# Fewer, larger transposing transfers in a fused attention and token-mixing kernel: z by overlapping twos, the last row block by two groups, keys by the stretch

## The chip, the cores and the metric

The kernel runs on one core of one Trainium2 chip. The metric is the device time of one execution in microseconds (us), lower is better; several executions are timed and their median is taken. One more execution is recorded by the hardware profiler, and every row of a profile below is of such an execution. PE is the matmul engine (PEld its weight loads), DVE, ACT and POOL are the vector, scalar and general engines, and SP issues most of the DMA transfers.

## What is computed

Eight batches of 3200 rows; u and v have 256 columns, z has 64.

```python
def _attn_ref(u, v, z):
    scale = 1.0 / S
    scores = scale * np.matmul(z, z.transpose(0, 2, 1))
    attn = np.maximum(scores, 0.0) ** 2
    out = np.matmul(attn, v)
    return u * out                       # this is x of the second part

def _moe_ref(x, w_q, w_k, w_out):
    wq = x @ w_q                         # queries, 64 columns
    wk = x @ w_k                         # keys, 64 columns
    W_tok = (1 / sqrt(64)) * np.einsum('bsd,btd->bst', wq, wk)
    mixed = np.einsum('bst,btd->bsd', W_tok, x)
    return np.maximum(mixed, 0.0) @ w_out
```

There is no softmax in either part. The second part is computed as queries times the small matrix "keys transposed times x" (64 x 256), which the kernel calls the heads.

## The kernel before

**Tiling.** A batch's 3200 rows are 25 row blocks of 128. They are grouped into seven groups: six of 512 rows (four blocks) and a last one of 128 rows (the row block 24, `LASTG`). A *tile* (b, gi, t) is the score block of row block t against the 512 (or 128) columns of group gi, after relu and square. Tiles are made in pairs: two score matmuls, one on the upper and one on the lower 64 rows of PE (`scores`, L224), into one PSUM tile; then relu on DVE or ACT (`first_stage`, L247 or L243); then the square on POOL or ACT into a buffer `at` (`second_stage`, L262 or L260), of which there are `NAT` = 15. Because two matmuls run side by side on 64 rows each, the turned z (`zT`) must hold the 64 values of z twice, in both halves of the 128 partitions.

**Symmetry.** The score matrix is symmetric, so the tile of group gi against block t also gives, transposed, the tile of t's group against gi's rows. For near groups (`is_turned`: at most two groups further, or the last group) the squared tile is transposed by a DMA on SP's queue (L282, buffers `tt1`, `tt2`, and `ttl` for the last row block) instead of being computed again. In the order of pairs, the tile of row block 24 stands as the last of a group's turned ones, paired with whatever comes next, and is transposed alone, 512 columns wide.

**Accumulation.** For each group the products of squares and v are added up in PSUM (`second_product`, L316), 10,000 matmuls of 64x256 in all. This is the bulk of PE's work. A finished group is multiplied by u (`gate`, L353), transposed by DMA (`turn_x`, L377), projected to queries and keys (L394), and cast to fp16 on ACT (L407) into `qk`, which holds queries in one half of the partitions and keys in the other, the halves swapped for the second half of a group.

**Keys and heads.** Each group's `qk` is transposed as a whole by one DMA (`turn_keys`, L412, 53 of them) although only its keys are used. When all groups of a stretch (groups 0 to 2, then 3 to 6) have their keys turned, the head products run on PE (`heads`, L421). After the second stretch the mixing of the batch (L457) and the output projection (L509) follow, among the next batch's work.

**z of the next batch.** `load_z` brings it densely on POOL's queue (with a cast to fp16); two DVE copies (`double_z`, L150, 128x1600 each) write every value twice, side by side; five transposing DMAs (`turn_z`, L156, five row blocks each) make `zT`. The first batch's z is doubled by casts and transposed on PE (L126) instead.

**Order.** The order of all instructions is written at build time by a planner inside the kernel. It keeps a clock for each engine and for SP and the DMA engines with assumed costs (for a transposing DMA, 1.28 us of SP and 0.21 us of DMA per row block), and chooses at each step between a new pair, a product that is ready, and extra work. `move(ready, due, issue, takes, ...)` queues a DMA for SP with a time from which it may go and one by which it is due. On the chip each engine then runs its list in that order and waits on semaphores. SP issues in order as well: a transfer that waits for its data holds everything behind it.

Of the kernel before, what the change touches and what calls it, by code (L numbers as in the profile page):

```python
# [9 lines left out]
FP16 = mybir.dt.float16  # L10
# [6 lines left out]
def kernel(  # L17
# [37 lines left out]
    NK = 5  # L55

    consts = ctx.enter_context(tc.tile_pool(name="consts", bufs=1))
    pz = ctx.enter_context(tc.tile_pool(name="pz", bufs=1))
# [3 lines left out]
    pk = ctx.enter_context(tc.tile_pool(name="pk", bufs=NK))  # L62
# [7 lines left out]
    pq = ctx.enter_context(tc.tile_pool(name="pq", bufs=10))  # L70
# [16 lines left out]
    zT, vs, us, xs, xTs, qks, ks, hacc, hx, hss, rts, zds = ({} for _ in range(12))  # L87
# [9 lines left out]
    zd0 = pz.tile([P, NT, 2, dqk], FP16, tag="zd", name="zd")  # L97
    vs[0] = pv.tile([P, NT, D], FP16, tag="v_sb", name="v_sb")
    zT[0] = pzt.tile([P, S], FP16, tag="zT2", name="zT2")
# [41 lines left out]
    zdense, ztimes = {}, []  # L141

    def load_z(b):
        zdense[b] = pz.tile([P, NT, dqk], FP16, tag="zn", name="zn")
        nc.gpsimd.dma_start(out=zdense[b][:], in_=rows(z, b))

    def double_z(b, half):
        if half == 0:
            zds[b] = pz.tile([P, NT, 2, dqk], FP16, tag="zd", name="zd")
        nc.vector.tensor_copy(out=zds[b][:, :, half, :], in_=zdense[b][:])  # L150

    def turn_z(b, i):
        ztimes.append((b, i))
        if i == 0:
            zT[b] = pzt.tile([P, S], FP16, tag="zT2", name="zT2")
        nc.sync.dma_start_transpose(  # L156
            out=zT[b][:].rearrange("p (n s) -> p n s", s=P)[:, 5 * i : 5 * i + 5, :],
            in_=zds[b][:, 5 * i : 5 * i + 5, :, :].rearrange("p n a k -> p (n a k)"),
        )

# [33 lines left out]
    def is_turned(gi, gj):  # L194
        return gi < gj and (gj <= gi + FAR or gj == LASTG)
# [4 lines left out]
    tiles, ends = [], {}  # L200
    for b in range(B):
        for gi in range(NG):
            near = [t for t in range(NT) if is_turned(gi, group_of(t))]
            own = [
                t for t in range(NT) if t not in near and not is_turned(group_of(t), gi)
            ]
            if b == 0 and gi == 0:
                order = own + near
            elif len(tiles) % 2:
                order = own[:1] + near + own[1:]  # L210
            else:
                order = near + own
            tiles += [(b, gi, t) for t in order]
            ends[b, gi] = len(tiles)
    NTILE = len(tiles)
    NPAIR = NTILE // 2
    made, turned = {}, {}

    def scores(p):
        assert len(ztimes) >= 5 * tiles[2 * p + 1][0] and p_chunk(p) in z_at, (p, clock, len(ztimes), z_at)  # L220
        sc = ps_tile("sc")
        for h, (b, gi, ti) in enumerate(tiles[2 * p : 2 * p + 2]):
            gs, gw = starts[gi], widths[gi]
            nc.tensor.matmul(  # L224
                out=sc[:, h, 0:gw],
                lhsT=zT[b][top(h), ts(ti, P)],
                rhs=zT[b][top(h), ds(gs, gw)],
                start=True,
                stop=True,
            )  # L230
        return sc
# [21 lines left out]
    def second_stage(p, g, on_act):  # L253
        at = pat.tile([P, 2 * W], FP16, tag="at", name="at")
        at0 = 0
        for hs, w in pieces(p):
            n = hs.stop - hs.start
            out = at[:, at0 : at0 + n * w].rearrange("p (n w) -> p n w", w=w)
            if on_act:
                nc.scalar.square(out=out, in_=g[:, hs, 0:w])  # L260
            else:
                nc.gpsimd.tensor_mul(out=out, in0=g[:, hs, 0:w], in1=g[:, hs, 0:w])  # L262
            at0 += n * w
        at0, blocks = 0, []
        for tile_ in tiles[2 * p : 2 * p + 2]:
            b, gi, ti = tile_
            made[tile_] = (at, at0)
            gj = group_of(ti)
            if is_turned(gi, gj):
                blocks.append((b, gi, gj, ti - starts[gj] // P, 1, at0, at0 + widths[gi]))  # L270
            at0 += widths[gi]
        if len(blocks) == 2 and blocks[0][:3] == blocks[1][:3] and blocks[1][3] == blocks[0][3] + 1:
            blocks = [blocks[0][:4] + (2, blocks[0][5], blocks[1][6])]

        def turn(b, gi, gj, n0, nn, c0, c1):
            if (b, gi, gj) not in turned:
                kind, nr, bufs = ("l", 1, 8) if gj == LASTG else (gj - gi, 4, gj - gi + 2)
# [4 lines left out]
            nc.sync.dma_start_transpose(out=out[:, 4 * n0 : 4 * (n0 + nn), :], in_=at[:, c0:c1])  # L282

        return [(x, lambda x=x: turn(*x)) for x in blocks]


# [3 lines left out]
    def weights(b, gi, ti, j):  # L290
        if (b, gi, ti) in made:
            at, at0 = made[b, gi, ti]
            return at[:, ds(at0 + j * P, P)]
        gj = group_of(ti)
        return turned[b, gj, gi][:, j, ti - starts[gj] // P, :]
# [33 lines left out]
    def gate(g):  # L329
# [4 lines left out]
        if b == B - 1 and gi == GRAM:  # L334
            spare = pz.tile([P, NT, 2, dqk], FP16, tag="zd", name="xd")
            spare = spare[:].rearrange("p n a k -> p (n a k)")
# [64 lines left out]

    def projections_out(b, gi, ps):
        xTs.pop((b, gi))
        n = min(2, widths[gi] // P)
        qks[b, gi] = pq.tile([P, 2, HW], FP16, tag="qk", name="qk")
        nr = len(halves(gi))
        nc.scalar.copy(out=qks[b, gi][:, 0:nr, 0 : n * P], in_=ps[:, 0:nr, 0 : n * P])  # L407

    def turn_keys(b, gi):
        nn = widths[gi] // P  # L410
        ks[b, gi] = pk.tile([P, 4, 2, dh], FP16, tag="kx", name="kx")
        nc.sync.dma_start_transpose(  # L412
            out=ks[b, gi][:, 0:nn, :, :].rearrange("p n a h -> p n (a h)"),
            in_=qks[b, gi][:].rearrange("p r s -> p (r s)")[:, 0 : nn * P],
        )

    def heads(b, gis, ps):
        todo = [(gi, n) for gi in gis for n in range(widths[gi] // P)]
        for i, (gi, n) in enumerate(todo):
            for r in range(2):  # L420
                nc.tensor.matmul(  # L421
                    out=ps[top(i % 2), r, 0:D],
                    lhsT=ks[b, gi][top(r), n, 1 - n // 2, :],
                    rhs=x_rows(b, gi, n)[top(r), :, :],
                    start=(i < 2),
                    stop=(i >= len(todo) - 2),
                )
        for gi in gis:
            del xs[b, gi], ks[b, gi]
# [23 lines left out]
    def mix(b, gi, banks):  # L453
        n = min(2, widths[gi] // P)
        for db in range(ND):
            for r in halves(gi):
# [3 lines left out]
                    rhs=qks[b, gi][top(r), r, 0 : n * P],  # L460
# [233 lines left out]
    def block_landed(t, p, b, gi, gj, nn):  # L694
# [5 lines left out]
        if blocks[b, gi, gj] == widths[gj] // P:  # L700
            for n in range(widths[gi] // P):
                row_at[b, gj, starts[gi] // P + n] = t + 0.5

    def use_keys(b, gi):
# [7 lines left out]
        n = widths[gi] / P  # L712
        if b < last or gi < GRAM:
# [4 lines left out]
        close_slot(slot, done)  # L718

    FIRST_HEADS = range(3)  # L720

    def keys_landed(b, gi):
        keyed.append((b, gi))
        for gis in FIRST_HEADS, range(3, NG if b < last else GRAM):
            if gi in gis and all((b, i) in keyed for i in gis):
                add_extra(clock[PE] + 0.5, "heads", lambda gis=gis: use_heads(b, gis))

    def use_heads(b, gis):
# [7 lines left out]
        if gis is FIRST_HEADS:  # L736
            return
# [73 lines left out]
    def batch_begun(b, t):  # L811
        if b + 1 < B:
            t += 6 if b == 0 else 0
            at_time(t + 6, lambda: (load_z(b + 1), push(3.0)))
            for half in range(2):
                at_time(
                    t + 18 + 3 * half,
                    lambda half=half: (double_z(b + 1, half), give(DVE, clock[PE], 0.98)),
                )
            for i in range(5):  # L820
                move(t + 24 + 6 * i, t + 40 + 6 * i, 1.28, 1.05, lambda i=i: turn_z(b + 1, i))
# [147 lines left out]

    make_identity(nc, ident)  # L970
# [31 lines left out]
    while stages or work:  # L1002
# [18 lines left out]
        able = p < NPAIR and z_at[p_chunk(p)] <= now and (p < NAT or all_used(p - NAT) and turned_at.get(p - NAT, 0.0) <= now and not out_of.get(p - NAT))  # L1021
# [131 lines left out]
```

## Time and profile before

| | us |
|---|---|
| median of three timed runs | 775.47 |
| lowest and highest | 773.03, 776.76 |
| the profiled execution | 773.32 |
| its span, first to last instruction | 771.5 |
| granted clock of PE, share | 0.998 |
| PE busy in the span | 753.5 |
| POOL, ACT, DVE busy | 563.9, 496.7, 461.4 |

The profile is of one execution. Its page gives busy time by engine, the chain of work that ended last, and groups of instructions by source line; each group's row has count, busy time, the mean of one in ns, and the idle time of the engine before them with what ended it. Further views list waits, DMA transfers with the time from issue to landing, and the instructions in order of time.

### The profile page before, as it was taken

How to read it: one execution, taken by the hardware profiler on the slowest of the kernel's cores; microseconds unless marked ns; L12 is line 12 of the kernel's file. 1: busy time of each engine (PE TensorE's matmuls, PEld its weight loads, DVE VectorE, ACT ScalarE, POOL GpSimd, SP SyncE). 2: the span in 40 equal slices, each digit the busy share in tenths (PEclk: the TensorE clock that was granted, in tenths of full speed). 3: DMA queues.
4: the chain of work that ended last, by engine and by line, in shares of the span. 5: the costliest groups of instructions: out<-in, count | busy, mean ns of one | idle time of the engine just before them, and what ended most of it. 6: DMA issues, size and time to landing. Idle time of an engine off the chain costs nothing.

```text
span 771.5 us, 28734 instructions
## 1 busy us (share of the span) xinstructions
PE 753.5 (98%) x12707; PEld 654.1 (85%) x12707; DVE 461.4 (60%) x496; ACT 496.7 (64%) x650; POOL 563.9 (73%) x363
## 2 busy tenths in 40 slices
PE   6999999999999999999999999999999999999996
PEld 4788889888888889988898898889988899888884
DVE  5675466555586465655556554755577756566544
ACT  5565766755676666777666666776657466775425
POOL 7896686885888477776788567875787768878840
PEclk9999999999999999999999999999999999999999
DMA  8899999999999999999999999999999999998636
GB/s 196 139 191 144 185 176 180 153 189 228 194 194 169 202 205 189 205 147 229 178 209 167 175 198 206 178 197 159 220 188 194 154 189 185 226 201 166 166 82 235
DMA packets 309806, 142.49 MB, mean 185 GB/s; under 512 B 287408, under 2 KB 291376, under 8 KB 309680
## 3 DMA queue, kind: packets, MB, share of 16 engines
q1 hardware_dynamic: 302624, 124.34, 88.7%
q0 software_dynamic: 6768, 15.98, 15.7%
q8 instruction: 99, 1.62, 0.9%
q10 hardware_dynamic: 288, 0.33, 0.1%
q14 instruction: 27, 0.22, 0.1%
HBM read 59.64 MB, written 26.21 MB: 111 GB/s over the span
## 4 chain that ended last, share of the span: by engine, by line
PE 91%; DMA 3%; DVE 2%; POOL 1%; issue 1%; SPq 1%; ACT 0%; DVEq 0%; POOLq 0%; ACTq 0%
PE acc L316 67%; PE sc L224 13%; PE fo L509 5%; PE qk L394 3%; PE hd L421 2%; DMA tt<-at 2%; PE mx L457 2%; DVE g L247 1%; PE fo L484 1%; DMA v_sb<-in_v_dram 1%; POOL at L262 1%; SPq L282 0%; DMA z<-in_z_dram 0%; DVE fo L557 0%; PE xtx L577 0%
## 5 line engine op out<-in xcount | busy, mean ns | idle before, releaser
L262 POOL TENSOR_TENSOR at<-g 128x1024 f16<-128x1024 f32 (+1 forms) x279 | 520.0, 1879 | 172.1 <-DVE g L247 125.0
L316 PE MATMUL acc<-v_sb,at 64*128 64x256 f16 x7312 | 494.8, 270 | 3.7 <-DMA v_sb<-in_v_dram 2.2
L247 DVE TENSOR_SCALAR g<-sc 128x1024 f32<-128x1024 f32 (+1 forms) x292 | 348.4, 1206 | 213.9 <-PE sc L224 197.4
L316 PEld LDWEIGHTS <-at 64*128 64x128 f16 x7312 | 387.1, 94 | 58.7 <-issue 5.0
L243 ACT ACTIVATE g<-sc 128x1024 f32<-128x1024 f32 (+2 forms) x176 | 173.1, 988 | 119.4 <-PE sc L224 107.3
L260 ACT ACTIVATE at<-g 128x1024 f16<-128x1024 f32 (+2 forms) x189 | 191.0, 1019 | 18.1 <-DVE g L247 14.8
L224 PE MATMUL sc<-zT 64*128 64x512 f16 x920 | 176.5, 380 | 2.9 <-DVE g L247 1.6
L316 PE MATMUL acc<-v_sb,tt 64*128 64x256 f16 x2304 | 167.3, 269 | 0.3 <-DMA tt<-at 0.3
L316 PEld LDWEIGHTS <-tt 64*128 64x128 f16 x2304 | 124.0, 94 | 16.7 <-issue 0.9
L353 DVE TENSOR_TENSOR x_sb<-acc,u_sb 128x512 f16<-128x512 f32 x92 | 59.0, 683 | 26.2 <-PE acc L316 23.2
L562 ACT ACTIVATE fo<-fo 128x1024 f32<-128x1024 f32 (+2 forms) x43 | 42.6, 999 | 37.0 <-PE fo L509 33.4
L224 PEld LDWEIGHTS <-zT 64*128 64x128 f16 x920 | 55.3, 94 | 12.9 <-issue 8.3
L474 ACT ACTIVATE rt<-mx 128x1024 f16<-128x1024 f32 (+1 forms) x49 | 44.8, 928 | 18.1 <-PE mx L457 17.9
L509 PE MATMUL fo<-wo,rt 64*128 64x256 f16 x668 | 52.2, 269 | 0.2 <-DVE g L247 0.2
L407 ACT CAST qk<-qk 128x512 f16<-128x512 f32 (+1 forms) x53 | 28.6, 540 | 25.5 <-PE qk L394 25.3
L509 PEld LDWEIGHTS <-rt 64*128 64x128 f16 x668 | 36.1, 94 | 3.3 <-issue 0.4
L303 ACT COPY sign<-sign 1x1 f32<-1x1 f32 x95 | 17.3, 182 | 31.9 <-PE acc L316 30.1
L394 PE MATMUL qk<-xT_sb,wqk 64*128 64x256 f16 (+1 forms) x396 | 31.0, 265 | 0.0
L316 PE MATMUL acc<-v_sb,ttl 64*128 64x256 f16 x384 | 27.2, 269 | 0.0
L394 PEld LDWEIGHTS <-wqk 64*128 64x128 f16 x416 | 22.3, 94 | 1.9 <-issue 0.2
L316 PEld LDWEIGHTS <-ttl 64*128 64x128 f16 x384 | 20.5, 94 | 2.7
L526 DVE COPY sign<-sign 1x1 f32<-1x1 f32 x31 | 4.4, 141 | 29.9 <-PE fo L509 29.7
(54 smaller groups left out, 204.4 us busy)
## 6 DMA issues: line engine op xcount, KB each, us to landing
u_sb<-in_u_dram SPq DMA_DIRECT2D x48, 512.0 KB, 5.0
out_dram<-fo SPq DMA_DIRECT2D x47, 512.0 KB, 4.3
v_sb<-in_v_dram POOLq DMA_DIRECT2D x35, 320.0 KB, 6.4
zn<-in_z_dram POOLq DMA_DIRECT2D x7, 400.0 KB, 6.3
tt<-at SPq DMA_TRANSPOSE x144, 4.8
u_sb<-in_u_dram SPq DMA_DIRECT2D x8, 128.0 KB, 4.1
hx<-ha SPq DMA_DIRECT2D x16, 64.0 KB, 3.5
xT_sb<-x_sb SPq DMA_TRANSPOSE x56, 4.9
```

The costliest lines, as they stand in the source:

```text
L224: nc.tensor.matmul(out=sc[:, h, 0:gw], lhsT=zT[b][top(h), ts(ti, P)], rhs=zT[b][top(h), ds(gs, gw)], start=True, stop=True,)
L243: nc.scalar.activation(out=g[:, hs, 0:w], in_=sc[:, hs, 0:w], func=RELU, scale=GSCALE)
L247: nc.vector.tensor_scalar(out=g[:, hs, 0:w], in0=sc[:, hs, 0:w], scalar1=0.0, scalar2=GSCALE, op0=AOP.max, op1=AOP.mult,)
L260: nc.scalar.square(out=out, in_=g[:, hs, 0:w])
L262: nc.gpsimd.tensor_mul(out=out, in0=g[:, hs, 0:w], in1=g[:, hs, 0:w])
L316: product = nc.tensor.matmul(out=g["acc"][k][:, ds(j * D, D)], lhsT=weights(b, gi, ti, 2 * k + j if whole else 0)[top(r), :], rhs=vs[b][to ...
L353: nc.vector.tensor_mul(out=out, in0=g["acc"][k][:].rearrange("p (m d) -> p m d", d=dh), in1=u2.rearrange("p n (c d) -> p (n c) d", d=dh),)
L394: nc.tensor.matmul(out=ps[:, r, 0 : n * P], lhsT=wqk[top(r), c, :, :].rearrange("p t h -> p (t h)"), rhs=xTs[b, gi][top(r), 0:n, c, :], st ...
L407: nc.scalar.copy(out=qks[b, gi][:, 0:nr, 0 : n * P], in_=ps[:, 0:nr, 0 : n * P])
L474: nc.scalar.activation(out=out, in_=ps[:, 0:nr, 0 : ND * n * P], func=RELU)
L509: product = nc.tensor.matmul(out=ps[:, bank, ds(j * D, D)], lhsT=flat[top(r), ds((dc * n + j) * P, P)], rhs=wo[top(r), dc, :], start=(stag ...
L562: nc.scalar.mul(out=flat_out[:, sl], in_=part, mul=FINAL_SCALE)
```

## The change

Three pieces, all on what SP issues as transposing transfers.

*z.* The dense z gets a zeroed row block on either side (`zn`, 27 blocks of 64 columns, one buffer in place of `zn` and the doubled `zd`). A transfer over 26 neighbouring blocks is read as 13 pairs of blocks; its transpose puts the first of each pair into the upper half of the partitions and the second into the lower. One transfer starts at block 0, one at block 1, so that every row block lands once in each half. In the upper half each block stands one place further (`z_cols` adds it; `zT` is 128 columns longer). The DVE copies are dropped. Each transfer has 13 blocks of 128x128; there are two a batch instead of five.

*The last row block.* Its tiles of two neighbouring groups (gi even, gi + 1) are made as one pair at the end of the even group's list, in a buffer of its own (`atl`, one buffer beside the 15 of `at`), and transposed together by one transfer of 1024 columns. A pair may be made when the pair that last had its buffer is used and turned (`heirs`, `free_of`).

*Keys.* The casts of a whole stretch go into one tile. When all its groups are cast, two transfers, one for each half of the groups, transpose only the 64 rows that hold keys. There are 32 of them.

The space of the dropped buffers goes to these; the first batch's doubled z lies in a buffer of v, and the spare of the last batch's end in one of zT.

```diff
+    zn = consts.tile([P, NT + 2, dqk], FP16, tag="zn", name="zn")
     def load_z(b):
-        zdense[b] = pz.tile([P, NT, dqk], FP16, tag="zn", name="zn")
-        nc.gpsimd.dma_start(out=zdense[b][:], in_=rows(z, b))
-
-    def double_z(b, half):
-        if half == 0:
-            zds[b] = pz.tile([P, NT, 2, dqk], FP16, tag="zd", name="zd")
-        nc.vector.tensor_copy(out=zds[b][:, :, half, :], in_=zdense[b][:])
+        nc.gpsimd.dma_start(out=zn[:, 1 : NT + 1, :], in_=rows(z, b))
 
     def turn_z(b, i):
...
         nc.sync.dma_start_transpose(
-            out=zT[b][:].rearrange("p (n s) -> p n s", s=P)[:, 5 * i : 5 * i + 5, :],
-            in_=zds[b][:, 5 * i : 5 * i + 5, :, :].rearrange("p n a k -> p (n a k)"),
+            out=zT[b][:].rearrange("p (n two s) -> p two n s", two=2, s=P)[:, i, :, :],
+            in_=zn[:, i : i + NT + 1, :].rearrange("p n k -> p (n k)"),
         )
+    def z_cols(b, h, n0, n):
+        return ds((n0 + (1 if b and h == 0 else 0)) * P, n)
...
+            if gi % 2 == 0 and gi < LASTG:
+                at = len(order) - (len(tiles) + len(order)) % 2
+                order[at:at] = [(b, gi, LAST), (b, gi + 1, LAST)]
+            tiles += order
...
+    def of_two(p):
+        return tiles[2 * p][2] == LAST and tiles[2 * p + 1][2] == LAST and tiles[2 * p][1] < LASTG
+    heirs = {}
+    for some, n in (
+        ([p for p in range(NPAIR) if not of_two(p)], NAT),
+        ([p for p in range(NPAIR) if of_two(p)], 1),
+    ):
+        for i, p in enumerate(some):
+            heirs[p] = some[i - n] if i >= n else None
...
     def second_stage(p, g, on_act):
-        at = pat.tile([P, 2 * W], FP16, tag="at", name="at")
+        tag, bufs = ("atl", 1) if of_two(p) else ("at", NAT)
+        at = pat.tile([P, 2 * W], FP16, tag=tag, name="at", bufs=bufs)
...
-    def turn_keys(b, gi):
-        nn = widths[gi] // P
-        ks[b, gi] = pk.tile([P, 4, 2, dh], FP16, tag="kx", name="kx")
+    def turn_keys(b, i, gis, r):
+        n = sum(min(2, widths[gi] // P) for gi in gis if r in halves(gi))
+        if (b, i) not in ks:
+            ks[b, i] = pk.tile([P, 2, 7, dh], FP16, tag="kx", name="kx")
         nc.sync.dma_start_transpose(
-            out=ks[b, gi][:, 0:nn, :, :].rearrange("p n a h -> p n (a h)"),
-            in_=qks[b, gi][:].rearrange("p r s -> p (r s)")[:, 0 : nn * P],
+            out=ks[b, i][:, r, 0:n, :], in_=qks[b, i][top(1 - r), r, 0 : n * P]
         )
...
+        for r in range(2):
             move(
-                done + SLACK, done + 10.0, 1.28, 0.21 * n, lambda: turn_keys(b, gi),
-                lambda t: at_time(t, lambda: keys_landed(b, gi)), lambda: len(ks) < NK,
+                done + SLACK, done + KDUE, 1.28, 0.65, lambda r=r: turn_keys(b, i, gis, r),
+                lambda t, r=r: at_time(t, lambda: keys_landed(b, gis, r)), lambda: len(ks) < 2 or (b, i) in ks,
             )
...
-            for i in range(5):
-                move(t + 24 + 6 * i, t + 40 + 6 * i, 1.28, 1.05, lambda i=i: turn_z(b + 1, i))
+            for i in range(2):
+                move(t + 24 + 14 * i, t + 45 + 14 * i, 1.28, 2.73, lambda i=i: turn_z(b + 1, i))
...
+    for i in (0, NT + 1):
+        nc.gpsimd.memset(zn[:, i, :], 0.0)
```

More of the change, by code (lines that the diff above doesn't have):

```diff
@@ L85 @@
     ctx.enter_context(tc.manual_schedule())
-    zT, vs, us, xs, xTs, qks, ks, hacc, hx, hss, rts, zds = ({} for _ in range(12))
+    zT, vs, us, xs, xTs, qks, ks, hacc, hx, hss, rts = ({} for _ in range(11))
     def rows(t, b):
@@ L294, in weights @@
         gj = group_of(ti)
+        if gi == LASTG:
+            return turned[b, gj - gj % 2, gi][:, gj % 2, ti - starts[gj] // P, :]
         return turned[b, gj, gi][:, j, ti - starts[gj] // P, :]
@@ L400, in projections, with stretch_of, queries @@
                 )
+    STRETCHES = [range(3), range(3, NG)]
+    def stretch_of(gi):
+        return next(i for i, gis in enumerate(STRETCHES) if gi in gis)
+    def queries(b, gi):
+        i = stretch_of(gi)
+        at = (gi - STRETCHES[i][0]) * HW
+        return qks[b, i][:, :, ds(at, min(HW, widths[gi]))]
     def projections_out(b, gi, ps):
@@ L699, in block_landed @@
         blocks[b, gi, gj] = blocks.get((b, gi, gj), 0) + nn
-        if blocks[b, gi, gj] == widths[gj] // P:
-            for n in range(widths[gi] // P):
-                row_at[b, gj, starts[gi] // P + n] = t + 0.5
+        if gj == LASTG or blocks[b, gi, gj] == widths[gj] // P:
+            n0 = starts[gi] // P
+            for n in range(n0, n0 + (8 if gj == LASTG else 4)):
+                row_at[b, gj, n] = t + 0.5
     def use_keys(b, gi):
@@ L735, in use_heads @@
         close_slot(slot, done)
-        if gis is FIRST_HEADS:
+        if gis[0] == 0:
             return
@@ L968, in all_used, with free_of @@
         return all(x in used for x in tiles[2 * p : 2 * p + 2])
+    for i in (0, NT + 1):
+        nc.gpsimd.memset(zn[:, i, :], 0.0)
+    def free_of(p, now):
+        return p is None or all_used(p) and turned_at.get(p, 0.0) <= now and not out_of.get(p)
     make_identity(nc, ident)
@@ L1020 @@
         p = produced[0]
-        able = p < NPAIR and z_at[p_chunk(p)] <= now and (p < NAT or all_used(p - NAT) and turned_at.get(p - NAT, 0.0) <= now and not out_of.get(p - NAT))
+        able = p < NPAIR and z_at[p_chunk(p)] <= now and free_of(heirs[p], now)
         wanted = able and p * total < (done_acc[0] + lead) * NPAIR
```

106 lines of the change are left out of this document (56 added, 50 removed).

## The prediction

> **What bounds the kernel now.** I read the page first, then the busy time of each engine by stretch, then the chain that ended last, then SP's queue.
>
> ```profile
> span 771.5 us, 28734 instructions
> ...
> PE 753.5 (98%) x12707; PEld 654.1 (85%) x12707; DVE 461.4 (60%) x496; ACT 496.7 (64%) x650; POOL 563.9 (73%) x363
> ...
> PE 91%; DMA 3%; DVE 2%; POOL 1%; issue 1%; SPq 1%; ACT 0%; DVEq 0%; POOLq 0%; ACTq 0%
> ...
> L262 POOL TENSOR_TENSOR at<-g 128x1024 f16<-128x1024 f32 (+1 forms) x279 | 520.0, 1879 | 172.1 <-DVE g L247 125.0
> ...
> L247 DVE TENSOR_SCALAR g<-sc 128x1024 f32<-128x1024 f32 (+1 forms) x292 | 348.4, 1206 | 213.9 <-PE sc L224 197.4
> ```
>
> TensorE is busy for 753.5 of 771.5 us and carries 91% of the chain. The stretches show where the other 18.0 us lie; the columns are the stretch, its length, and busy time with instruction counts of PE, PEld, DVE, ACT and POOL.
>
> ```profile
> core 0: us, PE busy (x) PEld busy (x) DVE busy (x) ACT busy (x) POOL busy (x), PEclk, DMA share, GB/s
> 0.00:40.00 40.00, 31.57 (x407) 22.62 (x409) 24.56 (x26) 22.59 (x26) 32.44 (x33) 1.00 0.84 167
> 40.00:60.00 20.00, 19.91 (x336) 15.99 (x336) 13.71 (x13) 13.04 (x17) 19.75 (x16) 1.00 1.12 198
> 60.00:88.00 28.00, 28.00 (x488) 23.49 (x484) 14.45 (x14) 15.09 (x20) 16.09 (x10) 1.00 1.13 159
> 88.00:150.00 62.00, 61.67 (x1054) 53.40 (x1050) 40.11 (x44) 44.30 (x55) 49.12 (x33) 1.00 1.13 173
> 150.00:178.00 28.00, 28.00 (x491) 23.99 (x489) 13.27 (x15) 15.88 (x24) 20.27 (x13) 1.00 1.10 176
> 178.00:235.00 57.00, 56.92 (x982) 49.09 (x979) 37.91 (x41) 39.84 (x53) 46.77 (x29) 1.00 1.16 208
> 235.00:269.00 34.00, 34.00 (x592) 28.65 (x590) 15.71 (x18) 21.43 (x28) 22.88 (x15) 1.00 1.14 185
> 269.00:740.00 471.00, 468.60 (x8073) 418.07 (x8071) 288.37 (x312) 311.09 (x409) 353.08 (x214) 1.00 1.07 187
> 740.00:771.50 31.50, 24.80 (x322) 18.83 (x317) 13.34 (x17) 13.40 (x26) 3.49 (x5) 0.94 0.50 172
> ```
>
> From 40 to 740 us PE lacks 0.09 + 0 + 0.33 + 0 + 0.08 + 0 + 2.40 = 2.90 us in all. 8.43 us are missing before 40 us and 6.70 after 740. So there is little to win in waiting; the question is whether busy PE is working at its rate.
>
> ```profile
> 123.05 1.42 PE acc L316 x26
> ...
> 597.39 5.46 PE acc L316 x100
> ```
>
> Products of the accumulation stand in the chain at 1.42 / 26 = 54.6 ns and 5.46 / 100 = 54.6 ns each, far apart in time: the work itself runs at one rate. The Trainium skill (Perfetto Trace Analysis, Identifying the Most-Contended Engine) holds matmul busy time for a poor measure of headroom and prefers the share of weight loading. By that rule, with 85%, some 15% (115 us) might still be there; the equal rate of the two rows of the chain speaks against it, so I give it no case of its own above 0.01.
>
> **The change, part by part.** Counts below are read from the order of the built instructions, before against after.
>
> *TensorE.* The same 12,705 matmuls in the same shapes; only their order moves. Tail after the last accumulation: the same sequence. Term: 0.
>
> *SP's queue.* It issues 66 transposing transfers less: z 35 to 14, keys 53 to 32, last row block 48 to 24.
>
> ```profile
> L156 SPq DMA_TRANSPOSE zT<-zd x35: 1219/1331/2625, 56.1 to 638.5; - x35
> DMA to landing us min/median/max: 2.6/5.0/8.1
> L412 SPq DMA_TRANSPOSE kx<-qk x53: 1120/1238/3383, 68.8 to 735.1; - x53
> DMA to landing us min/median/max: 2.4/4.4/8.5
> L282 SPq DMA_TRANSPOSE tt<-at x144: 1231/1323/4969, 19.3 to 711.2; - x144
> L282 SPq DMA_TRANSPOSE ttl<-at x48: 1188/1296/3477, 34.8 to 727.3; - x48
> ```
>
> By the medians that frees 21 x 1.331 + 21 x 1.238 + 24 x 1.296 = 85 us of SP, about 11 per batch. It matters because SP is late at a batch's end, issuing back to back:
>
> ```profile
> 79.11 1.33 SPq L156 DMA_TRANSPOSE zT<-zd  x1
> 80.53 1.44 SPq L282 DMA_TRANSPOSE ttl<-at  x1
> 82.07 1.26 SPq L412 DMA_TRANSPOSE kx<-qk  x1
> 83.38 1.27 SPq L156 DMA_TRANSPOSE zT<-zd  x1
> 84.76 1.92 SPq L377 DMA_TRANSPOSE xT_sb<-x_sb  x1
> ```
>
> ```profile
> 87.11 0.38 PE L224 MATMUL sc<-zT 64*128 64x512 f16 x2
> 87.33 1.47 PE L316 MATMUL acc<-v_sb,at 64*128 64x256 f16 x24
> ...
> 89.62 0.60 PE L224 MATMUL sc<-zT 64*128 64x128 f16 x4
> ```
>
> Two score matmuls take 87.33 - 87.11 = 0.22 us, 0.11 each. In the written order the fifth z transfer stands 326 accumulation products, 21 scores and 8 others ahead of the next batch's first score: 326 x 0.0546 + 21 x 0.11 + 8 x 0.054 = 20.5 us of PE work. In the trace it is issued at 83.38 and that score starts at 89.62, 6.2 us later: SP is 14 us behind. Taking 11 us from it per batch should leave 0 to 4 us. But in these very stretches (60 to 88, 150 to 178, 235 to 269) PE is busy 28.00 of 28, 28.00 of 28 and 34.00 of 34: relief there buys no PE time by itself. What it can take away is the 2.90 us of the middle and the part of the start that is not fixed.
>
> ```profile
> 0.75 0.20 POOL masks.py:197 MEMSET ident<- 128x128 f16 x1 [0.29 <-POOLq L1137]
> ...
> 3.98 0.50 POOL L120 CAST zd<-z 128x384 f16<-128x384 f32 x1 [1.72 <-DMA z<-in_z_dram]
> 4.43 0.54 POOL L108 DMA_DIRECT2D v_sb<-in_v_dram  x1
> ```
>
> ```profile
> PE ztp L126 <- ACT zd L120: 4.2, 1, 4.2
> ...
> PE acc L316 <- DMA v_sb<-in_v_dram: 2.2, 1, 2.2
> PE sc L224 <- DVE g L247: 1.6, 3, 1.0
> ```
>
> At the start 4.2 us wait for z and 2.2 for the second v load (issued at 4.43); both stay. So 8.43 - 6.4 = 2.0 us there and 2.9 in the middle, 4.9 us, are open: that is the bound of the gain. For how much goes, the order gives a hint. I count PE work, at the prices above, from the end of a score pair to the first product that uses its squares. The path in between takes at least 1.206 + 1.879 = 3.1 us (DVE, then POOL) before handoffs. Of 428 pairs beyond the first 40 us of work 58 had under 4.5 us before and 19 have it after; the median goes from 8.3 to 10.2. The 14 DVE copies that doubled z go too:
>
> ```profile
> L150 DVE COPY zd<-zn 128x1600 f16<-128x1600 f16 x14 | 13.6, 974 | 0.0
> ```
>
> DVE is off the path (60% busy; PE waited 1.6 us for it at scores), so they are within the same 4.9. Term: -2.5, half of it; bounds 0 and -4.9.
>
> *Zeroed borders.* Two memsets of 128x64 on POOL ahead of the identity, each below the 0.20 us of the 128x128 one. Behind them stand the identity (PE needs it only when z is cast, at 4.2) and POOL's first cast, which waited 1.72 us for z anyway; that hides both. Without that cover, 0.4. Term: +0.1.
>
> *z in two transfers of 13 blocks.* 26 blocks a batch instead of 25, so the DMA engines carry the same. The new wait: the first score of a batch needs both transfers. In the new order the second stands 19 us of PE work ahead of it in the tightest batch (267 products, 20 scores, 42 others), 23 to 37 in the other six. Even SP 4 us late and the longest z landing, 8.1, plus as much again as the 2.6 of the quickest for its greater size, make 14.7. Term: 0; if SP stays 14 us late, 24.7 against 19, 23.9 and 23.4 costs 5.7 + 0.8 + 1.3 = +7.8.
>
> *The last row block's pairs* share one buffer. In 13 of 23 places the next such pair's scores are put 0.2 us of PE work behind the last product that uses the buffer, and all later pairs queue behind it. As counted above the later pairs still come earlier for their products than before; the four tightest beyond such a place have 3.3 to 4.2 us against the 3.1 us path. Term: 0; bounds 0 and +1.5.
>
> *Keys.* This part can lose. Before, each group's keys were turned as soon as cast; now both halves wait for the whole stretch, and the head products come soon after. From the issue of the second half to the first head product the new order has, over 16 stretches, 8.7 (134 products and 13 scores), 9.3, 9.6, 10.5, 11.0, 11.2, 11.3 and 11.6 us of PE work; the other eight have 13.9 and more. A head product that waits holds PE itself, and everything in its queue. Needed: lateness of SP plus landing. With the median landing of 4.4 and 0 to 4 us of lateness that is 4.4 to 8.4, under all sixteen. Needs of 9.5 cost 0.8 + 0.2 = 1.0; of 10.5, 1.8 + 1.2 + 0.9 = 3.9; of 12.5 (4 late and the 8.5 of the slowest landing, each time) 16.8. No trace here shows a transfer of 64 rows; I take the 128-row landing, as a half has 6 or 7 blocks of half height where a group had 4 whole ones. Term: +0.7; bounds 0 and +16.8.
>
> The Trainium skill speaks against this piece (DMA: Bandwidth & Descriptors, Rules for kernel authors): two transfers to disjoint partition halves serialize, and one over 128 partitions should be used. By that rule the second half lands later by all of the first one's time, an issue of 1.2 us, which makes 9.6 of the need of 8.4 and about +1.2 in place of +0.7.
>
> Sum: -2.5 + 0.1 + 0 + 0 + 0.7 = -1.7. The profiled execution took 773.32 us (span 771.5 and 1.8 around it), so 771.6 for one like it. The three timed runs have their median at 775.47, 2.15 above it; so 773.8 us is forecast for the median. A measurement of this kernel can tell about 0.5%, 3.9 us.
>
> **Rivals.**
>
> *All waits go (faster).* For it: SP loses a seventh of its issues, pairs come earlier. Runs of one program spread from 773.0 to 776.8 with the same work, so waits must differ between them, and the 2.15 us might go as well. Against it: where SP was latest PE waited for nothing. It gives 775.47 - 4.9 = 770.6, and 768.4 with the 2.15. Chance 0.30.
>
> *Keys come too late (slower).* One mechanism: SP, in order, issues both halves behind transfers that wait for their squares, and head products stall PE. It decides from a need of 10.5 us on (+3.9), that is SP 6 us late at a median landing; at 11.5 it is 2.8 + 2.2 + 1.9 + 1.0 + 0.5 + 0.3 + 0.2 = +8.9, so 773.8 - 0.7 + 8.9 = 782.0. For it: the 14 us of lateness seen at 83.38. Against: most of that is taken away. Chance 0.17; with z late (+7.8) or the shared buffer, slower has 0.23.
>
> *It does not do what it says.* If a 64-row transfer occupies the queue like a whole one, keys land about 1 us later: a need of 9.5, +1.0 and 774.1. It stays within no change.
>
> **How the numbers follow.** Forecast and last rival, no change within 0.5%: 0.47, from 771.6 to 779.3. Faster 0.30, slower 0.23. The range takes the low end of the faster case, 768.0, and the slower one up to a need of 11.5, 782.0; what lies beyond (needs of 12.5, z at 14 us late) has some 0.15.
>
> **What would show it.** Right: PE busy stays near 753.5; the middle from 40 to 740 us lacks less than 2.9; no wait of head products on key transfers; SP has gaps before a batch's end, and the z transfers are issued over 15 us ahead of the next batch's first score. Wrong: a wait of PE at the head products or at a batch's first score, or landings of the key halves above 6 us in the median.

## The result, and the profile after

The changed kernel takes 769.87 us (median of 8 runs, 768.81 to 772.56), the kernel before 774.28 us (median of 8, 772.01 to 776.76). The ratio is 0.9944 [0.9927, 0.9961]: 4.4 us, or 0.56%, less. The forecast was 773.8, no change within 0.5%, with 771.6 to 779.3 as its own stretch; what came is below it and beside the faster rival, 770.6.

The profiled execution is the slowest of the eight, 772.56 us, 2.7 above the median, so it shows the change on a bad day. From its page (span, busy time, chain by engine):

```profile
span 770.7 us, 28594 instructions
...
PE 752.6 (98%) x12707; PEld 656.9 (85%) x12707; DVE 470.6 (61%) x501; ACT 479.3 (62%) x626; POOL 565.6 (73%) x370
...
PE 87%; DMA 3%; POOL 3%; DVE 3%; ACT 2%; issue 1%; SPq 1%; POOLq 0%; DVEq 0%; ACTq 0%
```

TensorE has the same 12,707 matmuls and the same busy time as before, within 0.9 us. The chain goes through PE for 87% of the span, before 91%, and key transfers are new among its waits. From the list of waits of PE, and from the timeline around that wait:

```profile
PE ztp L126 <- ACT zd L120: 4.2, 1, 4.2
PE hd L463 <- DMA kx<-qk: 2.5, 2, 2.3
...
PE acc L343 <- DMA v_sb<-in_v_dram: 0.5, 1, 0.5
```

```profile
271.20 3.15 SPq L454 DMA_TRANSPOSE kx<-qk  x2
...
278.72 1.00 PE L463 MATMUL hd<-x_sb,kx 64*64 64x256 f16 x24 [2.32 <-DMA kx<-qk]
```

SP issues both key halves of the stretch back to back from 271.20 on, the second is there at 278.7, and PE stood for 2.32 us before the head products. That is the slower rival's mechanism, at one place of sixteen. Now busy time and matmul counts of the middle, 40 to 740 us, and of the stretch with that wait: the kernel before first, then the changed one.

```profile
40.00:740.00 700.00, 697.10 (x11987) 612.68 (x11987) 423.53 (x454) 460.67 (x600) 527.95 (x327) 1.00 1.09 186
240.00:340.00 100.00, 99.68 (x1720) 87.27 (x1718) 60.30 (x68) 70.54 (x90) 72.75 (x45) 1.00 1.10 188
```

```profile
40.00:740.00 700.00, 695.59 (x11980) 615.20 (x11978) 432.20 (x459) 441.83 (x575) 529.74 (x329) 1.00 1.05 182
240.00:340.00 100.00, 96.76 (x1667) 87.17 (x1663) 60.50 (x67) 60.10 (x80) 78.13 (x50) 1.00 1.08 187
```

Read the count in brackets: how many matmuls PE started in the same time. From 240 to 340 us the changed kernel does 53 fewer, which at 697.10 / 11987 = 58.2 ns each is 3.1 us behind. Over the whole middle it is only 7 behind, so in the other 600 us it is 46 ahead, 2.7 us. By idle time alone the changed kernel looks worse, 700 - 695.59 = 4.41 us in the middle against 2.90. The profile therefore holds a loss in the stretch with the wait and a gain outside it; the experiments part the two.

Transfers, from the views of the tiles (issue time least/median/longest in ns, first and last issue; time to landing):

```profile
L454 SPq DMA_TRANSPOSE kx<-qk x32: 1167/1500/2380, 84.1 to 736.6; - x32
...
L153 SPq DMA_TRANSPOSE zT<-zn x14: 1304/2491/5653, 61.4 to 624.8; - x14
...
DMA to landing us min/median/max: 3.9/6.6/10.4
...
L307 SPq DMA_TRANSPOSE ttl<-at x24: 1235/2017/5142, 33.8 to 729.4; - x24
...
L307 SPq DMA_TRANSPOSE tt<-at x144: 1232/1478/6075, 18.2 to 715.0; - x144
```

Fewer transfers, but each holds SP longer in this profile. By the medians SP spent 144 x 1.323 + 53 x 1.238 + 48 x 1.296 + 35 x 1.331 = 365 us on these four before, and 144 x 1.478 + 32 x 1.500 + 24 x 2.017 + 14 x 2.491 = 344 now: about 21 us freed, not 85. Medians leave out the long issues. Adding up every transposing issue of the traces, those for x included, gives 553 us before, 531 here and 501 in the profile of a later order of the changed kernel (e10 below): 22 to 52 us freed, depending on the order and the run.

### The profile page after: what moved, and what is told of

It reads as the page before. It is cut to its first block, busy times and chain, and to the rows that moved or that the text cites. A ratio compares the mean times of both kernels' runs of the same rounds, so it can differ in the third digit from the quotient of the medians.

```text
span 770.7 us, 28594 instructions
## 1 busy us (share of the span) xinstructions
PE 752.6 (98%) x12707; PEld 656.9 (85%) x12707; DVE 470.6 (61%) x501; ACT 479.3 (62%) x626; POOL 565.6 (73%) x370
## 4 chain that ended last, share of the span: by engine, by line
PE 87%; DMA 3%; POOL 3%; DVE 3%; ACT 2%; issue 1%; SPq 1%; POOLq 0%; DVEq 0%; ACTq 0%
PE acc L343 64%; PE sc L244 11%; PE fo L552 5%; POOL at L283 3%; PE qk L420 3%; DVE g L267 2%; DMA kx<-qk 2%; PE hd L463 2%; PE mx L500 1%; PE fo L527 1%; DMA v_sb<-in_v_dram 1%; ACT g L263 1%; ACT at L281 1%; DMA hx<-ha 0%; DMA z<-in_z_dram 0%
## 5 line engine op out<-in xcount | busy, mean ns | idle before, releaser
L267 DVE TENSOR_SCALAR g<-sc 128x1024 f32<-128x1024 f32 (+2 forms) x309 | 367.6, 1203 | 166.2 <-PE sc L244 153.7
L343 PEld LDWEIGHTS <-at 64*128 64x128 f16 x7312 | 391.8, 94 | 52.8 <-issue 3.3
L263 ACT ACTIVATE g<-sc 128x1024 f32<-128x1024 f32 (+2 forms) x159 | 157.0, 991 | 110.4 <-PE sc L244 100.0
L281 ACT ACTIVATE at<-g 128x1024 f16<-128x1024 f32 (+1 forms) x184 | 189.8, 1036 | 44.2 <-DVE g L267 41.6
L244 PE MATMUL sc<-zT 64*128 64x512 f16 x920 | 180.4, 379 | 1.5 <-DVE g L267 1.0
L343 PE MATMUL acc<-v_sb,tt 64*128 64x256 f16 x2304 | 165.5, 269 | 0.0
```

Source lines behind the costliest of these rows:

```text
L244: nc.tensor.matmul(out=sc[:, h, 0:gw], lhsT=zT[b][top(h), z_cols(b, h, ti, P)], rhs=zT[b][top(h), z_cols(b, h, gs // P, gw)], start=True, ...
L263: nc.scalar.activation(out=g[:, hs, 0:w], in_=sc[:, hs, 0:w], func=RELU, scale=GSCALE)
L267: nc.vector.tensor_scalar(out=g[:, hs, 0:w], in0=sc[:, hs, 0:w], scalar1=0.0, scalar2=GSCALE, op0=AOP.max, op1=AOP.mult,)
L343: product = nc.tensor.matmul(out=g["acc"][k][:, ds(j * D, D)], lhsT=weights(b, gi, ti, 2 * k + j if whole else 0)[top(r), :], rhs=vs[b][to ...
```

## The experiments

The theories. **Q**: SP's queue is relieved, and the time follows the transfers taken off it. **E**: score pairs come earlier ahead of their products. **K**: key halves that land late make the head products wait, a loss. **R** (first called L): any new order moves the time by some us, and this one is lucky. **S**: the gain belongs to the three pieces together, in whatever order.

### One piece undone, or one alone

e1: the keys group by group again, the rest of the change kept (291 transposes instead of 270; before 336).

```
-    qks[b, i] = pq.tile([P, 2, cols], ..., tag=f"qk{i}", name="qk")
+    qks[b, gi] = pq.tile([P, 2, HW], FP16, tag="qk", name="qk")
-    out=ks[b, i][:, r, 0:n, :], in_=qks[b, i][top(1 - r), r, 0 : n * P]
+    out=ks[b, gi][:, 0:nn, ...], in_=qks[b, gi][:]...[:, 0 : nn * P]
```

> The changed kernel with its keys turned group by group as before (53 whole transfers again, 291 in all); z and the last row block stay changed. Theory Q (SP's queue: the gain follows the number of transfers taken from it): 21 of the 66 come back, so a third of the 4.4 us is lost, about 771.3. Theory E (pairs made earlier for their products, 58 tight pairs down to 19): the order has 27 tight pairs, so at most 1 us is lost, 770 to 771. Theory K (late halves make head products wait): the head products no longer wait on keys and it is faster than the changed kernel, 768 to 769. Theory L (any reordering moves the time by a few us, no piece counts): anywhere from 769 to 775.

e2: the last row block as before, z and keys as changed (294 transposes).

```
-            if gi % 2 == 0 and gi < LASTG:
-                order[at:at] = [(b, gi, LAST), (b, gi + 1, LAST)]
+            near = [t for t in range(NT) if is_turned(b, gi, group_of(t))]
```

> The changed kernel with the last row block's tiles made and turned one by one as before (48 transfers again, 294 in all, 15 buffers and none beside them); z and keys stay changed. Theory Q: 24 of 66 come back, about 1.6 us lost, 771.5. Theory E: tight pairs rise from 19 to 37, so about half of the gain is lost, 772. Theory L: anywhere from 769 to 775.

e3: the kernel before with the z piece alone (315 transposes).

```
-            for i in range(5):
-                move(t + 24 + 6 * i, t + 40 + 6 * i, 1.28, 1.05, lambda i=i: turn_z(b + 1, i))
+            for i in range(2):
+                move(t + 24 + 14 * i, t + 45 + 14 * i, 1.28, 2.73, lambda i=i: turn_z(b + 1, i))
```

> The kernel before with the z piece alone (21 transfers and the 14 doubling copies on DVE gone, 315 transfers). Theory Q: a third of the gain, about 772.8. Theory E: 50 tight pairs against 58, so almost no gain, 773.5 to 774. Theory L: anywhere from 769 to 775.

e4: the kernel before in another order, nothing else.

```
-    lead = 140
+    lead = 144
```

> The kernel before with one number of the planner changed (lead 140 to 144), which reorders the work without touching any transfer or buffer; it has 63 tight pairs. Theories Q and E: no gain, 774 to 775. Theory L: up to 4 us away from before, either way.

Measured: e1 774.26 us, ratio to before 1.0003 [0.9991, 1.0015]; e2 775.27, 1.0017 [1.0002, 1.0032]; e3 774.20, 1.0006 [0.9992, 1.0019]; e4 776.87, 1.0029 [1.0012, 1.0045]; before, beside them, 774.28. None of e1 to e3 is faster than before, though they carry 45, 42 and 21 of the 66 transposes saved: Q, read as so much per transfer, had wanted 771.3, 771.5 and 772.8 and finds no support. E read by counting tight pairs finds none either (27, 37 and 50 pairs of under 4.5 us against 58 before and 19 after). K misses with e1, whose heads do not wait for keys: it had wanted 768 to 769. But e4 shows that order alone can cost 2.6 us, nearly as much as Q wanted for a piece, so one order of each does not rule these theories out. In the one profile of each, other waits of PE stand out than in the profile before (e1, e2, e3):

```profile
PE sc L245 <- DVE g L268: 4.5, 6, 1.5
```

```profile
PE sc L239 <- DVE g L262: 3.6, 6, 1.8
...
PE mx L489 <- DVE g L262: 1.8, 2, 1.3
```

```profile
PE sc L240 <- DVE g L263: 2.1, 8, 0.5
PE hd L439 <- DMA kx<-qk: 1.8, 1, 1.8
```

Scores waited 1.6 us for VectorE before; in e1 and e2 it is 4.5 and 3.6, much of it from stalls of 1.5 to 1.8 us (two in e1, one in e2) whose origin is told at the end. So each of these orders has its own stalls of some us, and they may hide what a piece brings. That asked for more than one order of each kernel.

### Luck of the order, or the change: the same nudge to both kernels

e5 and e6: one number of the planner moved, in the changed kernel and in the kernel before.

```
-    BIAS = 0.2
+    BIAS = 0.25
```

> The change as it is, and one number of the planner moved, BIAS 0.20 to 0.25 (by how much ScalarE must be free earlier to be given a stage). It removes and adds nothing; it only shifts the order of the stages a little. Theory S (the 4.4 us belong to the three pieces together, 66 transposes fewer and pairs made earlier, whatever the order): 769.5 to 771.5, and 3 to 6 us below the same nudge of the kernel before. Theory R (they belong to this one order, in which VectorE's small additions happen not to meet GpSimd's squares): the time goes back to 773 to 776, no better than the nudged kernel before.

> The kernel before, with the same number moved, BIAS 0.20 to 0.25. Theory S: 774 to 777, 3 to 6 us above the nudged changed kernel. Theory R: anywhere from 772 to 777, and it does not stand clearly above the nudged changed kernel.

e7 and e8: another number, in both.

```
-    LANDS = 4.0
+    LANDS = 4.1
```

> The change as it is, and another number of the planner moved, LANDS 4.0 to 4.1 (after how long a transfer counts as landed). Nothing is removed or added. Theory S: 769.5 to 771.5. Theory R: 773 to 776.

> The kernel before, with LANDS moved from 4.0 to 4.1. Theory S: 774 to 777, 3 to 6 us above the changed kernel with the same nudge. Theory R: 772 to 777, within 2 us of it on either side.

Measured, before beside them 774.25: e5 775.08 us (769.58 to 782.04; 774.46 without that longest run), ratio 1.0014 [0.9989, 1.0038]; e6 775.26, 1.0014 [0.9995, 1.0032]; e7 768.23 (766.86 to 769.07), 0.9925 [0.9908, 0.9942]; e8 774.84, 1.0014 [0.9996, 1.0032]. One pair says S (6.6 us apart), the other R (0.2 apart). The middle of e7, then of e8:

```profile
40.00:740.00 700.00, 698.89 (x12056) 612.04 (x12054) 438.40 (x466) 438.01 (x571) 532.61 (x331) 1.00 1.02 183
```

```profile
40.00:740.00 700.00, 694.69 (x11945) 608.57 (x11943) 426.02 (x457) 458.35 (x590) 516.20 (x322) 1.00 1.08 186
```

e7 starts 111 matmuls more, 6.5 us. What spoils e5 stands in its profile: windows first, then the timeline.

```profile
240.00:340.00 100.00, 97.41 (x1646) 86.04 (x1642) 66.03 (x68) 59.72 (x79) 72.21 (x44) 0.98 1.05 185
```

```profile
309.56 1.28 SPq L454 DMA_TRANSPOSE kx<-qk  x1
...
318.91 0.84 PE L463 MATMUL hd<-x_sb,kx 64*64 64x256 f16 x22 [2.15 <-DMA kx<-qk]
```

The second key half is issued at 309.56 and PE goes on with it at 318.91, 9.3 us later, where the median landing in this profile is 4.2. In that stretch e5 starts 1646 matmuls against 1724 of e7: 78, or 4.5 us. Idle time is 2.59 us against 0.14, which explains 2.45 of it. Most of the rest stands behind the wait, in the column of the granted clock (the first number behind the last bracket):

```profile
320.00:323.40 3.40, 3.40 (x32) 2.24 (x30) 2.11 (x4) 1.61 (x2) 1.89 (x1) 0.50 1.38 142
323.40:340.00 16.60, 16.35 (x278) 13.75 (x274) 12.79 (x12) 12.54 (x14) 12.36 (x8) 1.00 1.10 192
```

From 320.0 to 323.4 us the clock is 0.50; everywhere else in the middle of this profile it is 1.00. PE counts as busy all through, but it starts 32 matmuls at 106 ns each, where afterwards one takes 59. Half of 3.4 is 1.7 us, and 2.45 + 1.7 = 4.2 of the 4.5. That would be K at nearly twice the price of the wait, and it can be tested.

### Heads later, so that no key half can be late

e9 is e5 with this edit, e10 the changed kernel with it, e12 the kernel before with it.

```
-            add_extra(clock[PE] + 0.5, "heads", lambda: use_heads(b, gis))
+            add_extra(clock[PE] + 4.5, "heads", lambda: use_heads(b, gis))
```

> The nudged change of e5 (BIAS 0.25), with the heads due 4.5 us instead of 0.5 us after the second key half counts as landed; the shortest distance from that transfer's issue to the first head product is then 13.0 us of TensorE work instead of 9.0. Theory K (the changed order is worth its 4 to 6 us, and e5 lost them to key halves that landed late, as the 2.15 us wait at 317 us in its profile shows): 768.5 to 771.5, no head product waits for kx, and the spread of 12 us over its runs shrinks to 4. Theory R (the time goes by the order's luck): 773 to 777, whatever the heads do.

> The changed kernel with the heads due 4.5 us instead of 0.5 us after the second key half counts as landed (shortest distance 13.8 us instead of 8.7). Theory K: no wait for kx; 767.5 to 769.5, a little below the changed kernel's 769.87 since only some of its runs wait. Theory R: anything from 768 to 777. A rival of both, that late heads hold x and key buffers longer and push the mix against the end of the batch: 771 to 774 with waits of the mix products.

> The kernel before with the same late heads as e9 and e10 (due 4.5 us instead of 0.5 us after the last keys count as landed), and nothing else. It is the control: in the profile before no head product waits for keys, so under theory K there is nothing for it to win, 773.5 to 776, and the 5 to 6 us between it and e10 (768.81) are the change's own, with the late keys taken out. If the late heads themselves, not the change, make e9 and e10 fast (theory R, or a gain from spreading the work at a batch's end): 768 to 771.5.

Measured: e9 768.77 us, ratio to before 0.9944 [0.9911, 0.9977]; e10 768.81 (767.63 to 769.41), 0.9912 [0.9890, 0.9935], with before at 774.62; e12 776.01, 1.0027 [1.0011, 1.0044], with before at 773.98. In the profiles of e9 and e10 no head product waits for keys. Four microseconds more of distance bring e5 down by 6.3 us and the changed kernel by 1.1, which is less than two sessions can tell apart. They make the kernel before slower by 2.0, at the edge of what was expected: it had nothing there to win, and its order moved. The middle of e5, then of e9:

```profile
40.00:740.00 700.00, 694.62 (x11933) 619.75 (x11929) 446.78 (x465) 424.73 (x563) 534.03 (x326) 1.00 1.04 182
```

```profile
40.00:740.00 700.00, 699.45 (x12071) 615.46 (x12069) 459.78 (x486) 412.68 (x536) 549.75 (x341) 1.00 1.02 182
```

The middle of e10, then of e12:

```profile
40.00:740.00 700.00, 698.76 (x12060) 617.31 (x12056) 442.54 (x468) 432.71 (x567) 532.51 (x327) 1.00 1.03 183
```

```profile
40.00:740.00 700.00, 695.59 (x11949) 618.41 (x11951) 423.28 (x455) 460.40 (x592) 520.36 (x326) 1.00 1.09 186
```

So K is shown as a loss, but not for all of the 6.3 us. The profiled runs of e5 and e9 took 774.35 and 768.01. Of that, 2.15 us is the wait for keys and 1.7 the slower clock behind it, 3.9 together. The rest is other waits that e9's order does not have: scores for VectorE (2.8 us in e5, 0.8 in e9) and one projection for its transposed x (1.0). Later heads reorder the work as well, so that part may be R's.

S has the count of orders for it: five orders of the kernel before gave 774.3 to 776.9, five orders of the changed one 768.2 to 769.9 and, with late keys, 775.1. Two of these five, e9 and e10, were built to take the wait away; of the two blind nudges one kept the gain and one lost it. The change is worth 5.8 us where its keys are given time (e10 against before beside it), 7.2 against e12 with the same edit in another session. Through what it works is not shown: fewer issues, earlier pairs and the order itself all came together.

Two of the ten runs of e9 still took 775.0 and 778.6, so its spread is 10.6 us where 4 were expected. They have no profile, but their granted clock is on record: 0.993 and 0.994, in the other eight 0.997 to 0.999. A share of 0.004 is 3 us of 770, so they too lost part of their time to the clock. Whether a wait stood ahead of it is open.

### SP's load put back

e11: the changed kernel, with one transpose of a 128x128 constant into a scratch tile behind every sixth transfer that SP sends, 66 in all. The planner doesn't know of them, so the other engines keep their order.

```
         fn()
+        sent[0] += 1
+        if sent[0] % 6 == 0:
+            nc.sync.dma_start_transpose(out=idle[:, 0:1, :], in_=ident[:])
```

> The changed kernel, its order on every other engine untouched, with 66 transposes of one 128x128 block (of a constant, into a scratch tile that nothing reads) put on SP, one behind every sixth transfer: as many as the change takes away. Theory Q (the gain is SP's queue): the 4.4 us go again, 773 to 776, and products wait for transposed blocks or scores for z. Theory R and the theory that the pairs' order is what counts: 769.5 to 771.5, since the order is the same and a late block has some 10 us to spare. Theory K: late halves get later, 770.5 to 773, with head products waiting for kx at two or more batch ends.

Measured: 784.51 us (777.76 to 787.17), ratio to before 1.0101 [1.0059, 1.0143]. Every theory had too little. It costs 14.6 us against the changed kernel's 769.87, three times what the change had won. Its profile is of a run of 778.4 us, six below the median. The added tile's row, the waits of PE, and the middle:

```profile
L677 SPq DMA_TRANSPOSE idle<-ident x66: 1119/1187/2872, 21.8 to 759.8; - x66
```

```profile
PE hd L463 <- DMA kx<-qk: 4.4, 3, 2.6
...
PE acc L343 <- POOL at L283: 2.3, 3, 1.1
PE acc L343 <- DMA tt<-at: 1.7, 2, 1.0
```

```profile
40.00:740.00 700.00, 690.58 (x11868) 605.86 (x11866) 428.90 (x455) 441.03 (x572) 529.86 (x331) 1.00 1.08 185
```

66 x 1.187 = 78 us more on SP, and waits appear for keys (4.4), for transposed blocks (1.7) and for squares (2.3). The middle has 112 matmuls fewer than the changed kernel's (11980), 6.5 us; the two profiled runs are 778.4 - 772.56 = 5.8 us apart. The two longest of its six runs, 786.7 and 787.2, have a granted clock of 0.992 and 0.993, the two shortest 0.997 and 0.999, so the median holds time lost to the clock as well. So the queue does bear on the time. It doesn't do so in proportion, though: a load that the order was not written for costs 14.6 us, while orders that were written for 291, 315 and 336 transposes (e1, e3 and before) can't be told apart.

A version that beats both kernels: e7 (768.23) and e10 (768.81) are 5.8 to 6.0 us below before in their sessions. Below the changed kernel they are by 1 to 1.6 us, which is less than can be told here.

## Why the prediction was right, and where it was not

**TensorE, 0:** right. The same matmuls (12,707; the prediction's 12,705 is two short), busy time 752.6 against 753.5.

**SP's relief, -2.5, bounded by -4.9:** right in sign, too small. Two steps failed. First, "that frees ... 85 us of SP" counted old durations for new transfers; in the changed kernel's profile the larger ones hold SP 2.0 to 2.5 us at the median, and 22 us came free there, 52 in e10. SP was not 0 to 4 us late either:

```profile
75.10 1.89 SPq L153 DMA_TRANSPOSE zT<-zn  x1
...
86.36 0.40 PE L244 MATMUL sc<-zT 64*128 64x128 f16 x2
```

From the issue of the second z transfer to the next batch's first score it is 11.3 us in the changed kernel's timeline, where the order has at least 19 us of work in between: some 8 us late at this batch's end. Second, and worse, "4.9 us, are open: that is the bound of the gain". Against before, e10 starts 73 matmuls more in the middle, 4.2 us, while idle time there fell only from 2.90 to 700 - 698.76 = 1.24. The other 2.6 us came out of time that the record calls busy (698.76 / 12060 = 57.94 ns a matmul against 58.15). Priced by kind it is less: 77 products more at 0.0546 us and six scores fewer at 0.11 are 3.5 us of work and not 4.2, so about 2 us remain. The prediction had cited the rule against trusting that time and set it aside on two rows of 54.6 ns. The Trainium skill (Perfetto Trace Analysis, Identifying the Most-Contended Engine) calls matmul busy time a poor measure; by these counts it is right here, by about 2 us and not by the 115 that the share of weight loading would leave. A product counts as busy for 270 ns (the mean of L316 in the profile before) while the next one may start after 54.6, so a pause of up to 0.2 us between two of them is no idle time. Which pauses e10 has fewer of is not shown. Nor does busy time show a lower clock, which the last section comes back to.

**Zeroed borders, +0.1, and z, 0:** nothing here speaks against them. The v load behind the memsets came earlier in this profile (wait 0.5 us, before 2.2), and the start lacks 40 - 32.37 = 7.6 us against 8.4; e10 has 1.8 and 8.8, so neither is a gain. z transfers land in 6.6 us (median) and 10.4 at most, where 10.7 was allowed for, and no score waits for z. The mark of over 15 us from their issue to the first score was missed (the 11.3 above), without harm.

**The shared buffer, 0:** no wait of PE points to it (0.5 us for GpSimd's squares, before 0.7). It was not tried alone.

**Keys, +0.7, from 0 to +16.8:** the mechanism was named, and in this order the size of the term can't be told from zero; as a general figure it was too small. The halves land in 4.3 us at the median, as assumed and below the mark of 6. The tail decides: 9.3 us in e5, beyond the 8.5 that was taken as slowest. The changed kernel's profile has 2.5 us of waits for keys, at two head products, and its median lies 1.1 us above e10's (769.87 and 768.81), which is less than can be told. In e5 a stall of 2.2 us and the half clock behind it made 3.9; the prediction priced a wait at its own length. The Trainium skill's rule against two transfers to disjoint halves (DMA: Bandwidth & Descriptors, Rules for kernel authors) had given +1.2. A single transfer in their place was not tried, so the rule's own part is not shown.

**The cases:** the stated range held, 769.87 within 768.0 to 782.0, because it took in the low end of the faster rival; the likeliest case, 771.6 to 779.3 with a chance of 0.47, did not come. The forecast took half of a bound that was itself too low. The faster rival (0.30) came by its number, 770.6, and by a small margin. Its mechanism did not: in the changed kernel's profile the waits of the middle grew, from 2.90 to 4.41 us, and of the prediction's own signs the wait at the head products is one of being wrong. That the number fell so near is partly luck; the nudge of e5 alone would have put it back to 775.

**Open:** why e1, e2 and e3 gain nothing. Their profiles show stalls of their own, but other orders of them were not run, nor were they with late heads. What each piece brings by itself is therefore not settled.

## What to carry to other kernels

A kernel whose order is planned moves by some us with any edit: give the same harmless nudge to both versions, and compare several orders before a difference under 1% is put down to the edit. Count the matmuls started per stretch, and read the granted clock beside them, instead of adding up idle time; the idle time of a 98% busy engine was no bound on what could be won. When many small transfers become two late ones, move their reader by the tail of the landing, not by its median: 4 us of distance took away a wait that had cost 3.9 with what followed it. Give the control the same distance, for there it cost 2.0.

## What the runs showed of the hardware

A small VectorE addition with both inputs in SBUF, 0.42 us at its quickest, can take eight times as long beside GpSimd's squares. From the timelines of e1 and then e2:

```profile
323.11 3.75 POOL L284 TENSOR_TENSOR at<-g 128x1024 f16<-128x1024 f32 x2
...
323.83 3.32 DVE L467 TENSOR_TENSOR ha<-ha 128x256 f32<-128x256 f32 x1
...
328.34 0.39 PE L245 MATMUL sc<-zT 64*128 64x512 f16 x2 [1.47 <-DVE g L268]
...
336.56 2.48 DVE L477 TENSOR_TENSOR hs<-ha,hx 128x256 f16<-128x256 f32 x1
...
336.85 1.91 POOL L284 TENSOR_TENSOR at<-g 128x1024 f16<-128x1024 f32 x1
```

```profile
140.03 3.75 POOL L278 TENSOR_TENSOR at<-g 128x1024 f16<-128x1024 f32 x2
...
140.40 3.67 DVE L480 TENSOR_TENSOR hs<-ha,hx 128x256 f16<-128x256 f32 x1
...
145.26 0.39 PE L239 MATMUL sc<-zT 64*128 64x512 f16 x2 [1.76 <-DVE g L262]
```

At 323.83 in e1 and at 140.40 in e2, VectorE's addition starts while GpSimd squares, and ends 0.29 us after the second of two squares that follow each other without a gap (327.15 against 326.86, 144.07 against 143.78). The next first stage on VectorE comes late, and PE waits 1.5 and 1.8 us at a score. The Trainium skill (SBUF — State Buffer, Who interferes with whom) says that VectorE and GpSimd share a pair of ports under an exclusive lock, and that an operation which comes second is blocked in full; its summary names VectorE operations with two SBUF inputs among them. These two rows agree, and show that the block can last over two GpSimd instructions. The addition at 336.56 fits the order less clearly: it is recorded 0.29 us ahead of the square, while GpSimd was still issuing a transfer, and yet ends 0.28 us after that square. No run here took the additions off VectorE, so what that would save is open.

A wait of PE can cost more than its length. In e2, behind a wait of 1.76 us that ends at 145.26 and during a short one after it, the granted clock goes to half for 3.4 us, as it was behind e5's wait of 2.15:

```profile
146.20:149.60 3.40, 3.21 (x32) 2.62 (x33) 1.27 (x2) 2.14 (x4) 1.89 (x1) 0.50 1.20 202
```

Not every wait is followed by it. Behind 2.32 us in the changed kernel's profile, 2.58 in e11's and 1.47 in e1's the clock stayed at 1.00; what decides is not shown. The start of the kernel has the half rate too, and it ends at another time in each profile. Eight products in the profile before, then in e10's, each with what starts next:

```profile
14.51 1.09 PE L316 MATMUL acc<-v_sb,at 64*128 64x256 f16 x8
15.37 0.66 PE L224 MATMUL sc<-zT 64*128 64x512 f16 x2
```

```profile
13.37 0.61 PE L343 MATMUL acc<-v_sb,at 64*128 64x256 f16 x8
13.80 0.40 PE L244 MATMUL sc<-zT 64*128 64x512 f16 x2
```

They take 15.37 - 14.51 = 0.86 us in the one, 107 ns each, and 13.80 - 13.37 = 0.43 in the other, 54 each. The clock column does not show this, for the traces' clock records begin only at 16.9 and 8.9 us. So the two rows of 54.6 ns on which the prediction rested hold for their places and not for the start, and two profiles can differ there whatever the edit.

The other surprise is the price of SP's load: 66 transposes whose result nobody reads, 1.19 us each to issue, made the kernel 14.6 us slower.
